# A mixture-of-experts kernel: the instruction order of the first chunk's steps, with decoding, attention and x0's split moved

## The chip, the cores and the metric

One core of a Trainium2 chip. The metric is device time in microseconds (us) of one execution; the times shown are of single executions and their median. Engines: TensorE (PE), VectorE (DVE), ScalarE (ACT), GpSimd (POOL), and SyncE (SP), which only issues loads and stores here. Each engine runs its queue in order.

## The reference

```python
x = attention(q, k, v)              # 4 batches, 8 heads, 576 positions, 64 wide;
                                    # causal, each position sees the last 64
x = x.reshape(2304, 512)            # tokens by heads
h = x @ w_in                        # 512 -> 2048
g = where(h >= 1, h, where(h <= -1, 0, (h + 1)**2 / 4))
y = g @ w_out                       # 2048 -> 512
e, weight = top-1 of softmax(y @ w_gate + bias[modality])
out = weight * (relu(y @ w1[e]) @ w2[e])     # 8 experts, 512 -> 1024 -> 512
```

`w_in` and `w_out` come as 64-bit floats; the kernel turns their words into 32-bit floats itself.

## The kernel before

The 2304 tokens are taken in six chunks of 384. A chunk has 16 steps `f`, one for each 128 columns of the hidden layer: `l1(c, f)` multiplies the chunk's x by block f of `w_in` into PSUM, `relu` (two ACT instructions) and `act2` (one on DVE) make g of it, and `l2(c, f)`, two steps later, adds g times block f of `w_out` to three sums. While a chunk c is worked on, attention of chunk c+1 is made, six blocks of 64 positions with all heads. After the last chunk tokens are routed and the experts run. From the second chunk on weights and x are split into a high part and a rounded rest, and products are made of three matmuls.

The first chunk, `step0(f)` (L1048), has more to do than the others. Weights must be decoded, a pair of blocks at a time: `dec_load` (SP) fetches the pair's words, `dec_abs` (two on ACT), `dec_clamp` (four on DVE) and `dec_merge` (four on DVE) make 32-bit floats. `turn[f]` says which pairs step f decodes: one pair, and two in the steps of `TWICE` (L207); there are 16 pairs, the first of them ahead of step 0. `dec_load(p + 3)` is issued in the step that merges pair p, whose place it takes. Up to step 8 whole 32-bit weights and x0 are used (`l1_whole`, L476); from step `FS` = 9 on split ones, and from `FJ` = 10 on each step also makes the second chunk's first layer, `l1(1, f)`. `split_hi` (ACT) and `split_lo` (DVE) split a weight block; `soon` (L234 to L239) says in which step. `split_x0(j)` splits half j of x0: a copy on ACT (L349), the rest on DVE (L350).

Attention of the second chunk's blocks, numbered 6 to 11 here, is a pipeline over the steps: block 6 has phase 0 in step 1, phase 1 in step 2, and so on, block 7 one step later.

- Phase 0: `att_mm` (scores on PE, L370), `att_loads` (SP fetches later k and q), `att_max` (masked maxima, four on DVE, L385), `att_exp` (four exponentials with sums on ACT, L395).
- Phase 1: `load_v` (SP); `att_norm`, which is `att_sum` (two small instructions on DVE, L407 and L408) and `att_scale` (four on ACT for these blocks, L416).
- Phase 2: `att_tr`, four transposes on PE (L425) and a copy of the result, ts, on ACT (L430).
- Phase 3: `att_pv`, multiplication by v on PE (L447); `att_x`, xh on ACT (L467) and the rounded rest xl on DVE (L468).

Scores, transposes and products share three PSUM buffers ("aux"); s and ts have two buffers each, q, k and v two.

In the first chunk the order on PE, DVE, ACT and POOL is the order of the calls in `step0`, by `manual_schedule`; SP's order is written out by hand throughout. After the chunk a planner with estimated costs sets the order of DVE, ACT and POOL, and from step 3 of the second chunk PE's is by hand again.

Of the kernel before, what the change touches and what calls it, by code (L numbers as in the profile page):

```python
# [71 lines left out]
def moe_kernel(ctx, tc, qT, kT, v, w_in, w_out, mod, wg, wgT, mbias, w1, w2, cst, tri, empty, out, spec):  # L72
# [131 lines left out]
    PRE = 3  # L204
    LAG = 2
    FS, FJ = 9, 10
    TWICE = (3, 6)  # L207

    def part(kind, f, lo):
        return parts[kind, f][0][:, lo * WB : (lo + 1) * WB]  # L210
# [22 lines left out]
    NPR = len(pairs)  # L233
# [1 line left out]
    for f in range(FS, NF - 1):  # L235
        soon.setdefault(f + 1, []).append((1, f))
    soon[NF - 1].append((1, NF - 1))
    for f, kf in ((13, (0, 0)), (14, (0, 1)), (14, (0, 2)), (15, (1, 0))):
        soon[f].append(kf)  # L239
    turn, p = [], 1  # L240
    for f in range(NF + 1):
        turn.append(list(range(p, min(p + 1 + (f in TWICE), NPR))))
        p += len(turn[-1])
# [24 lines left out]
    def dec_abs(p, us=(0, 1)):  # L268
        if p < NPR:
            for u in us:  # L270
                dts.setdefault(p, {})[u] = tile_of([P, DM], f"dt{p}_{u}", I32, tag="y", bufs=4)
                A.activation(dts[p][u].bitcast(F32), words(p, u)[1].bitcast(F32), AF.Abs)

    def dec_clamp(p, us=(0, 1)):
        if p < NPR:
            t = dts[p]
            for u in us:
                tf = t[u].bitcast(F32)
                V.tensor_scalar(tf, tf, c0, c1, op0=ALU.max, op1=ALU.min)
            for u in us:  # L280
                V.tensor_scalar(t[u], t[u], 5, 2, op0=ALU.logical_shift_left, op1=ALU.logical_shift_right)

    def dec_merge(p, us=(0, 1)):
        if p < NPR:
            t = dts[p]
            for u in us:
                V.scalar_tensor_tensor(
                    t[u], words(p, u)[1], -0x40000000, t[u], op0=ALU.bitwise_and, op1=ALU.bitwise_or
                )
            for u in us:  # L290
                w = raw_home(p, u)
                V.scalar_tensor_tensor(
                    w, words(p, u)[0], 29, t[u], op0=ALU.logical_shift_right, op1=ALU.bitwise_or
                )
                whole[pairs[p][u]] = w.bitcast(F32)
# [46 lines left out]
    def split_x0(j):  # L342
        if not j:
            hi = [tile_of([P, 2 * WB], f"x0h{n}", F32R, tag=f"T{NF + 10 + n}") for n in range(2)]
            hi = [t[:, : KH * CT].rearrange("p (k n) -> p k n", k=KH) for t in hi]
            xs[0] = (hi, tile_of([P, KD, CT], "x0l", F32R, tag="xl", bufs=2))
        hi, lo = xs[0]
        ks = slice(j * KH, (j + 1) * KH)
        A.copy(hi[j], whole_x[0][:, ks])  # L349
        V.tensor_tensor(lo[:, ks], whole_x[0][:, ks], hi[j].bitcast(F32), op=ALU.subtract)  # L350
# [50 lines left out]
    def att_norm(i):  # L401
        att_sum(i)
        att_scale(i)

    def att_sum(i):
        sm = at[i][1]
        V.tensor_scalar_add(sm, sm, 1e-9)  # L407
        V.reciprocal(sm, sm)  # L408

    def att_scale(i):  # L410
        s, sm = at[i]
        s = s[:, :, : window(i)[0]]
        if BPC - 1 <= i < 2 * BPC:
            w = window(i)[0]
            for hp in range(KD):
                A.activation(s[:, hp, :w], s[:, hp, :w], AF.Copy, scale=sm[:, hp : hp + 1])  # L416
            return
        G.tensor_tensor(s, s, bc(sm, 2, window(i)[0]), op=ALU.mult)  # L418

    def att_tr(i):  # L420
        s, _ = at[i]
        n = window(i)[0]
        pt = aux([P, KD, P], f"pt{i}")
        for hp in range(KD):
            T.transpose(pt[:n, hp, :], s[:, hp, :n], C["ident"])  # L425
        if i < BPC:
            ts = lend(8 + i, 1).rearrange("p (k n) -> p k n", k=KD)
        else:
            ts = tile_of([P, KD, P], f"ts{i}", tag="ts", bufs=2)
        (V.tensor_copy if i < BPC - 2 else A.copy)(ts[:n], pt[:n])  # L430
        at[i] = ts

    def att_pv(i):
        o = 0
        if i < BPC:
            xo = ps.tile([P, KD, BLK], F32, name=f"xo{i}", tag="h", bufs=2)
        elif i < PAIRED:
            xo = aux([P, KD, BLK], f"xo{i}")
        else:
            o = i % GB  # L440
            xo = xos[i - 1] if o else aux([P, KD, GT], f"xo{i}")
        ts = at.pop(i)
        vt = vs.pop(i)
        w = window(i)[0]
        for hp in range(KD):
            for a in range(2):
                T.matmul(  # L447
                    xo[a * D : (a + 1) * D, hp, o * BLK : (o + 1) * BLK],
                    vt[:w, (2 * hp + a) * D : (2 * hp + a + 1) * D],
                    ts[:w, hp, a * BLK : (a + 1) * BLK],  # L450
                    start=True,
                    stop=True,
                )
        xos[i] = xo

    def att_x(i):
        xo = xos.pop(i)
        c, n = divmod(i, BPC)
        dst = slice(n * BLK, (n + 1) * BLK)
        if i >= PAIRED:  # L460
            xos.pop(i + 1)
            dst = slice(n * BLK, n * BLK + GT)
        if c == 0:
            A.copy(whole_x[0][:, :, dst], xo)
            return
        xh, xl = xs[c]
        A.copy(xh[:, :, dst], xo)  # L467
        V.tensor_tensor(xl[:, :, dst], xo, xh[:, :, dst].bitcast(F32), op=ALU.subtract)  # L468
# [14 lines left out]
    def l1(c, f):  # L483
        if (c, f) not in hs:
            if c == 1 and f >= FJ:
                hs[c, f] = aux([P, CT], f"h{c}_{f}")
            else:
                hs[c, f] = ps.tile([P, CT], F32, tag="h", name=f"h{c}_{f}", bufs=2)
            if c == 0 and f < FS:
                l1_whole(f, slice(0, CT))  # L490
        h = hs[c, f]
        n = 0
        for k in range(KD if c or f >= FS else 0):
            xh, xl = xs[c]
            xh = xh[:, k, :] if c else xh[k // KH][:, k % KH, :]
            for a, b in ((0, xh), (0, xl[:, k, :]), (1, xh)):
                T.matmul(h, wi(f, a)[:, k, :], b, start=n == 0, stop=n == 3 * KD - 1)  # L497
                n += 1

    def relu(c, f):  # L500
        h = hs[c, f]
        u = tile_of([P, CT], f"u{c}_{f}", tag="u", bufs=2)
        A.activation(u, h, AF.Relu, bias=half, scale=0.5)  # L503
        A.activation(u, u, AF.Square)  # L504
        us[c, f] = u
# [542 lines left out]
    def step0(f):  # L1048
        split0 = f - 1 >= FS
        join = f >= FJ  # L1050
        at_step = {f - st: BPC + k for k, st in enumerate(FIRST)}
        if f == NF - 3:
            free.extend(f"T{NF + k}" for k in (14, 15))
        if f >= 1:
            act2(0, f - 1)
            if split0:
                gsplit_hi(0, f - 1, us[0, f - 1])
        if f - 1 >= FJ:
            act2(1, f - 1)
        for kf in soon.get(f, []):  # L1060
            split_lo()
        if split0:
            gsplit_lo(0, f - 1, us[0, f - 1])
        for p in turn[f]:
            dec_clamp(p)
            dec_merge(p)
        if 3 in at_step:
            att_pv(at_step[3])
            att_x(at_step[3])
        if 2 in at_step:  # L1070
            att_tr(at_step[2])
        if 1 in at_step:
            load_v(at_step[1])
        if 0 in at_step:
            att_mm(at_step[0])
            att_loads(at_step[0])
        for p in turn[f]:
            dec_load(p + 3)
        l1(0, f)
        relu(0, f)  # L1080
        for p in turn[f + 1][:1]:
            dec_abs(p)
        if 1 in at_step:
            att_norm(at_step[1])
        if 0 in at_step:
            att_max(at_step[0])
            att_exp(at_step[0])
        if f in (FS - 2, FS - 1):
            split_x0(f - FS + 2)
        if join:  # L1090
            l1(1, f)
            relu(1, f)
        if f >= LAG:
            l2(0, f - LAG)
        for p in turn[f + 1][1:]:
            dec_abs(p)
        for kf in soon.get(f + 1, []):
            split_hi(kf)
        if f == FS - 1:
            token_bias()  # L1100
        if f == NF - 1:
            free.extend(f"T{NF + k}" for k in (10, 11))
            hold_back(gs[0, f - 1][0].bitcast(F32))
            wgb.append(tile_of([P, E, DM], "wgb", tag="dec"))
            SP.dma_start(
                wgb[0].rearrange("p e d -> p (e d)"),
                wgT.rearrange("(o e) d -> o (e d)", o=1).broadcast_to([P, E * DM]),
            )
# [7 lines left out]
    for n in range(len(its) + LAG):  # L1116
        c, f = its[n] if n < len(its) else (NC, n - len(its))
# [151 lines left out]
```

## Time and profile before

| what | us |
|---|---|
| median of 3 executions | 736.45 |
| lowest, highest | 735.43, 738.32 |
| the profiled execution, its own time | 735.82 |
| its span in the trace | 734.2 |
| PE busy in the span | 717.1 (98%) |
| DVE busy | 474.2 (65%) |
| ACT busy | 390.1 (53%) |

The profile is of one execution; its span is a little shorter than the time, which takes in start and end. Busy time of PE is that of pipelined matmuls, whose ends are modelled. The first chunk's steps 1 to 9 lie between 24 and 87 us, its last six until 126 us. In rows, `dt<-dec` on ACT is `dec_abs`, L279 and L281 are `dec_clamp`, L287 and L292 `dec_merge`, `g<-u,h` is `act2`, `u<-h,half` is the first instruction of `relu`.

### The profile page before, as it was taken

The page shows a single profiled execution, that of the slowest core. Times are in us where ns is not written, and L with a number is a line of the kernel's source. Part 1 is how long each engine was busy: PE and PEld are TensorE (multiplying, and loading weights), DVE is VectorE, ACT ScalarE, POOL GpSimd, SP SyncE. Part 2 cuts the span into 40 slices and gives each one's busy share as a digit, 9 for nine tenths or more (in the row PEclk, how much of TensorE's full clock was granted, in tenths as well). Part 3 has the DMA queues.
Part 4 walks back from the last instruction along what each step waited for, and adds up shares of the span by engine and source line. Part 5 has one row for each costly group of instructions (what it writes and reads, how often), then busy time and mean ns, then how long its engine had stood idle before and what let it go on. Part 6 is the DMA issues. An engine that isn't in the chain of part 4 may idle for free. (4 is left out here: it accounts for less than half of the span.)

```text
span 734.2 us, 12536 instructions
## 1 busy us (share of the span) xinstructions
PE 717.1 (98%) x4217; PEld 625.5 (85%) x4217; DVE 474.2 (65%) x1439; ACT 390.1 (53%) x942; POOL 127.0 (17%) x185
## 2 busy tenths in 40 slices
PE   8899999999999999999999999999999999999994
PEld 6555689888998989888989898999989989898984
DVE  5999897797397528852696638866775545453600
ACT  6777778666545535554555445645444544453511
POOL 3200000113001201120111502031058322201010
PEclk9999999999999999999999999999999999999998
DMA  9997413322121203220310015245455754444310
GB/s 327 334 346 258 147 55 127 118 66 80 52 86 59 80 15 108 73 80 16 108 59 29 2 41 171 67 93 191 158 137 171 232 181 155 159 159 160 115 43 7
DMA packets 48570, 89.26 MB, mean 122 GB/s; under 512 B 6976, under 2 KB 16320, under 8 KB 48368
## 3 DMA queue, kind: packets, MB, share of 16 engines
q1 hardware_dynamic: 44064, 78.36, 32.3%
q0 software_dynamic: 4288, 9.79, 4.6%
q8 instruction: 35, 0.57, 0.3%
q14 instruction: 39, 0.32, 0.1%
q10 hardware_dynamic: 144, 0.22, 0.1%
HBM read 78.89 MB, written 9.87 MB: 121 GB/s over the span
## 5 line engine op out<-in xcount | busy, mean ns | idle before, releaser
L497 PE MATMUL h<-xh,w 128*128 128x384 f32 x640 | 179.4, 341 | 0.0
L549 PE MATMUL py<-w,gh 128*128 128x512 f32 x522 | 162.1, 393 | 0.0
L497 PEld LDWEIGHTS h<-xh,w 128*128 128x128 f32 x640 | 117.1, 188 | 2.3
L549 PEld LDWEIGHTS py<-w,gh 128*128 128x128 f32 x522 | 96.6, 188 | 16.2
L497 PE MATMUL h<-xl,w 128*128 128x384 f32 x320 | 107.4, 336 | 0.0
L796 DVE TENSOR_TENSOR e<-wr,e 128x512 fp32r<-128x512 f32 x112 | 74.7, 690 | 45.2 <-ACT e L795 43.2
L549 PE MATMUL py<-w,gl 128*128 128x512 f32 x261 | 102.7, 396 | 0.0
L858 PE MATMUL hp<-zh,e 128*128 128x384 f32 x384 | 100.9, 336 | 0.0
L503 ACT ACTIVATE u<-h,half 128x384 f32<-128x384 f32 x96 | 55.5, 578 | 82.3 <-PE h L497 70.8
L873 PE MATMUL yo<-e,hm 128*128 128x512 f32 x348 | 99.0, 394 | 0.0
L517 DVE SCALAR_TENSOR_TENSOR u<-u,h 128x384 f32<-128x384 f32 x81 | 44.7, 552 | 68.3 <-ACT u L504 67.8
L603 DVE CUSTOM_DVE_ANT_0 prod<-y,wgb 128x512 f32<-128x512 f32 x120 | 85.3, 710 | 1.3
L529 ACT CAST gh<-u 128x384 fp32r<-128x384 f32 x81 | 41.6, 514 | 67.5 <-DVE u L517 29.1
L795 ACT CAST e<-wr 128x512 fp32r<-128x512 f32 x112 | 66.0, 616 | 18.4 <-DMA wr<-in_w 18.2
L873 PEld LDWEIGHTS yo<-e,hm 128*128 128x128 f32 x348 | 64.2, 188 | 12.4
L858 PEld LDWEIGHTS hp<-zh,e 128*128 128x128 f32 x384 | 69.6, 188 | 0.8
L418 POOL TENSOR_TENSOR s<-s,sm 128x512 f32<-128x512 f32 (+1 forms) x24 | 26.2, 1093 | 222.4 <-DVE sm L408 158.1
L858 PE MATMUL hp<-zl,e 128*128 128x384 f32 x192 | 64.3, 335 | 0.0
L534 DVE TENSOR_TENSOR gl<-u,gh 128x384 fp32r<-128x384 f32 x81 | 45.5, 562 | 26.7 <-ACT gh L529 25.7
L497 PEld LDWEIGHTS h<-xl,w 128*128 128x128 f32 x320 | 60.2, 188 | 1.9
L549 PEld LDWEIGHTS py<-w,gl 128*128 128x128 f32 x261 | 48.9, 188 | 10.4
L395 ACT ACTIVATE s<-s,mx 128x128 f32<-128x128 f32 (+1 forms) x120 | 45.9, 385 | 11.7 <-DVE mx L385 11.7
(218 smaller groups left out, 1049.5 us busy)
## 6 DMA issues: line engine op xcount, KB each, us to landing
wr<-in_w SPq DMA_DIRECT2D x112, 256.0 KB, 2.9
q<-in_qT SPq DMA_DIRECT2D x32, 256.0 KB, 3.4
dec<-in_w_in SPq DMA_DIRECT2D x16, 512.0 KB, 5.5
dec<-in_w_out SPq DMA_DIRECT2D x16, 512.0 KB, 4.3
v<-in_v SPq DMA_DIRECT2D x27, 256.0 KB, 3.0
k<-in_kT SPq DMA_DIRECT2D x15, 384.0 KB, 4.7
yd<-y SPq DMA_DIRECT2D x18, 256.0 KB, 2.2
wgb<-in_wgT SPq DMA_DIRECT2D x1, 2048.0 KB, 6.9
```

The costliest lines, as they stand in the source:

```text
L395: A.activation(s[:, hp, :n], s[:, hp, :n], AF.Exp, bias=mx[:, hp : hp + 1], scale=-1.0, accum_out=sm[:, hp : hp + 1],)
L497: T.matmul(h, wi(f, a)[:, k, :], b, start=n == 0, stop=n == 3 * KD - 1)
L503: A.activation(u, h, AF.Relu, bias=half, scale=0.5)
L517: V.scalar_tensor_tensor(g, u, 1.0, h, op0=ALU.min, op1=ALU.max)
L529: A.copy(gh, u)
L534: V.tensor_tensor(gl, u, gh.bitcast(F32), op=ALU.subtract)
L549: T.matmul(ys[c][t], a[:, sl], wo(f, b), start=f == first and n == 0, stop=f == last and n == 2)
L603: V.tensor_tensor_reduce(prod, yt[t], wgb[0][:, e, :], 1.0, 0.0, ALU.mult, ALU.add, lg[:, t, e : e + 1])
L795: A.copy(wpart(i, p, 0), t)
L796: V.tensor_tensor(wpart(i, p, 1), t, wpart(i, p, 0).bitcast(F32), op=ALU.subtract)
L858: T.matmul(hp, w1s(i, f, k, a), b[:, k, :], start=n == 0, stop=n == 3 * KD - 1)
L873: T.matmul(yo, a[f][:, sl], w2s(i, f, b), start=n == 0, stop=n == 3 * NF2 - 1)
```

## The change

In `step0` the calls get another order. On DVE the clamps come first, then `att_sum`, then the rest xl of `att_x`, then the merges of the first pair; a second pair is decoded whole after them. On PE the order becomes: product with v, first layer of the first chunk, scores, transposes, (first layer of the second chunk), second layer. On ACT `att_scale` comes ahead of `relu` and `dec_abs`, the copy of the transposes after them. On SP the order is kept. Step 3 decodes one pair, no longer two, so pairs 5 to 7 and those from 9 on are decoded a step later than before. x0 is split in steps 6 and 7, formerly 7 and 8. Four weight blocks that the second chunk needs are split in steps 14, 14, 15, 15, formerly 13, 14, 14, 15.

```diff
-    TWICE = (3, 6)
+    TWICE = (6,)
...
-    for f, kf in ((13, (0, 0)), (14, (0, 1)), (14, (0, 2)), (15, (1, 0))):
+    for f, kf in ((14, (0, 0)), (14, (0, 1)), (15, (0, 2)), (15, (1, 0))):
...
-        for p in turn[f]:
+        dec_clamp(*turn[f][:1] or [NPR])
+        if 3 in at_step:
+            att_pv(at_step[3])
+        if 1 in at_step:
+            att_sum(at_step[1])
+        if 3 in at_step:
+            att_x(at_step[3])
+        if 1 in at_step:
+            att_scale(at_step[1])
+        dec_merge(*turn[f][:1] or [NPR])
+        for p in turn[f][1:]:
             dec_clamp(p)
             dec_merge(p)
-        if 3 in at_step:
-            att_pv(at_step[3])
-            att_x(at_step[3])
-        if 2 in at_step:
-            att_tr(at_step[2])
+        l1(0, f)
+        relu(0, f)
+        for p in turn[f + 1][:1]:
+            dec_abs(p)
         if 1 in at_step:
             load_v(at_step[1])
         if 0 in at_step:
...
         for p in turn[f]:
             dec_load(p + 3)
-        l1(0, f)
-        relu(0, f)
-        for p in turn[f + 1][:1]:
-            dec_abs(p)
-        if 1 in at_step:
-            att_norm(at_step[1])
+        if 2 in at_step:
+            att_tr(at_step[2])
         if 0 in at_step:
             att_max(at_step[0])
             att_exp(at_step[0])
-        if f in (FS - 2, FS - 1):
-            split_x0(f - FS + 2)
+        if f in (FS - 3, FS - 2):
+            split_x0(f - FS + 3)
```

## Rows read from the trace of the kernel before

**Rows 1.** Windows: stretch, busy us of each engine, PEclk, DMA share, GB/s.

```profile
27.63:87.46 59.83, 54.50 (x278) 31.38 (x276) 55.04 (x163) 45.29 (x128) 5.40 (x5) 1.00 0.77 281
87.46:125.91 38.45, 38.45 (x198) 34.81 (x196) 34.55 (x67) 29.05 (x57) 1.14 (x4) 1.00 0.26 100
```

**Rows 2.** Waits of PE to 140 us, then after it: total, times, longest.

```profile
PE pt L425 <- ACT s L416: 4.6, 3, 3.1
...
PE h L497 <- DVE x0l L350: 0.7, 1, 0.7
...
PE rt L907 <- ACT hr L901: 0.3, 1, 0.3
```

**Rows 3.** Timeline of PE: start us, length us, engine, line, operation.

```profile
36.91 1.20 PE L425 MATMUL pt<-cs,s 128*128 128x128 f32 x4 [3.09 <-ACT s L416]
...
53.19 0.69 PE L447 MATMUL xo<-ts,v 128*64 128x64 f32 x16
...
54.38 1.07 PE L370 MATMUL sc<-k,q 128*128 128x128 f32 x8
55.28 2.75 PE L476 MATMUL h<-x,raw 128*128 128x384 f32 x8
57.86 2.74 PE L543 MATMUL py<-raw,g 128*128 128x512 f32 x6
60.53 0.69 PE L447 MATMUL xo<-ts,v 128*64 128x64 f32 x16
...
81.46 0.69 PE L447 MATMUL xo<-ts,v 128*64 128x64 f32 x16
...
87.46 0.73 PE L497 MATMUL h<-x0h,w 128*128 128x384 f32 x1
```

**Rows 4.** Timeline of DVE, from steps 2, 3, 4 and 7.

```profile
32.30 0.76 DVE L279 TENSOR_SCALAR dt<-dt 128x512 f32<-128x512 f32 x2
...
33.64 1.29 DVE L287 SCALAR_TENSOR_TENSOR dt<-dec,dt 128x512 int32<-128x512 int32 x2
...
36.04 0.17 DVE L407 TENSOR_SCALAR sm<-sm 128x4 f32<-128x4 f32 x1
...
36.34 0.26 DVE L385 CUSTOM_DVE_ANT_0 s<-sc,cs 128x128 f32<-128x128 f32 x1
...
37.16 0.55 DVE L517 SCALAR_TENSOR_TENSOR g<-u,h 128x384 f32<-128x384 f32 x1
...
50.45 0.42 DVE L468 TENSOR_TENSOR xl<-xo,xh 128x256 fp32r<-128x256 f32 x1
...
76.74 0.96 DVE L350 TENSOR_TENSOR x0l<-x,x0h 128x768 fp32r<-128x768 f32 x1 [2.83 <-ACT x0h L349]
```

**Rows 5.** Timeline of ACT, from steps 3 to 5 and 7.

```profile
46.72 0.39 ACT L395 ACTIVATE s<-s,mx 128x128 f32<-128x128 f32 x1
...
48.27 0.35 ACT L467 CAST xh<-xo 128x256 fp32r<-128x256 f32 x1
48.52 0.57 ACT L430 COPY ts<-pt 128x512 f32<-128x512 f32 x1
50.72 0.58 ACT L503 ACTIVATE u<-h,half 128x384 f32<-128x384 f32 x1 [1.63 <-PE h L476]
...
51.76 1.23 ACT L272 ACTIVATE dt<-dec 128x512 f32<-128x512 f32 x2
52.88 1.28 ACT L416 ACTIVATE s<-s,sm 128x128 f32<-128x128 f32 x4
...
58.06 0.58 ACT L503 ACTIVATE u<-h,half 128x384 f32<-128x384 f32 x1 [1.85 <-PE h L476]
...
75.89 0.82 ACT L349 CAST x0h<-x 128x768 fp32r<-128x768 f32 x1
```

**Rows 6.** DMA issues, 10 to 60 us: times, KB each, us to landing.

```profile
q<-in_qT SPq DMA_DIRECT2D x7, 256.0 KB, 6.7
```

**Rows 7.** Windows, after the last matmul of the kernel.

```profile
730.00:734.20 4.20, 0.00 (x0) 0.00 (x0) 0.00 (x0) 0.00 (x0) 0.00 (x0) 0.50 0.00 0
```

## The prediction

> **What bounds the kernel now.** I read the windows first: which engine is full, stage by stage. From 87 us on TensorE (PE) has no gap [rows 1], and after 140 us it waits 0.3 us in all [rows 2]. So time won or lost in the first chunk of tokens, the stretch that the change reorders, comes out at the end almost unchanged, as long as nothing later starts to wait. In the first chunk PE is busy 54.50 of 59.83 us [rows 1]. The list of waits names the gaps: 4.6 us in three waits of the transposes for ScalarE's scaling, the longest 3.1 us, and 0.7 us for the rest of x0 [rows 2]. Some 1.5 us more hide in three groups of transposes that lasted 1.20 us because they ran head by head behind the scaling (one of the three: [rows 3]); a step without a wait gives multiplication by v and transposes together 1.19 us (53.19 to 54.38), about half for each. About 7 us is therefore all that an order can win here.
>
> The timeline shows the cause. The sums of a block stand on VectorE (DVE) behind the step's merges (36.04, after merges from 33.64) [rows 4]; the scaling and the next step's transposes wait for them, and behind the transposes wait the scores and the first-layer block.
>
> **Durations,** as distances between starts, of one profiled execution. PE, a step of 7.34 us (53.19 to 60.53): by v and transposes about 0.60 each, scores 0.90, l1 2.58, l2 2.67 [rows 3]. DVE: clamps of a pair 1.34, merges 2.40, sums 0.30, maxima of a block 0.82, rest 0.4 and x0's rest 0.9 (0.42 and 0.96 less overlap), g 0.47 (0.55 less the 0.08 by which neighbours overlap) [rows 4]. ScalarE (ACT): the four exponentials 1.55, xh 0.25, ts 0.5, relu 1.04 and starting 2.78 after l1 (55.28 to 58.06), abs of a pair 1.12, scaling 1.18, half of x0 0.72 (0.82 less overlap) [rows 5].
>
> **The change, walked through.** Total work is unchanged on every engine; only waits move. I carry the end of each link to the next; blocks of the second chunk are numbered 6 to 11.
>
> *Steps 2 to 5: a gain.* In step 2 the clamps end at 33.64, the sums of block 6 at 33.94 instead of 36.34, the merges at 36.34, the maxima of block 7 at 37.16, where they ended before. ACT: scaling 35.1, relu 36.2, abs 37.3, exponentials of block 7 38.9. PE no longer waits until 36.91 [rows 3]: it runs step 3 (l1, scores, transposes, l2: 6.75) from 33.8 to 40.5. But its next instruction, block 6 by v, needs ts of block 6, which now stands on ACT behind step 3's scaling, relu and abs: g 37.6, clamps 39.0, sums of block 7 39.3, scaling 40.5, relu 41.5, abs 42.7, ts 43.2. So PE waits from 40.5 to 43.3: the wait of 3.1 us comes back as one of 2.8. From there a step is PE's own 7.34, since each link of relu, abs and ts (l1 start + 2.78 + 1.04 + 1.12 + 0.5, so 6.1 after the step's start) comes before its end. Step 5 begins at 50.6, where it began at 53.19: **2.6 us won.** Taking the second pair out of step 3 leaves DVE at 5.7 us a step, which hides under PE; without that it would be 9.5 and not hide.
>
> *Steps 6 to 8: a loss.* Steps 6 and 7 begin on PE at 58.0 and 65.3; step 7 has no scores and is 6.44 us long, so PE is free at 71.8. DVE in step 6 has two pairs and, new here, half of x0. ACT, step 5: relu 55.1, abs 56.2, ts 56.7, exponentials of block 10 58.3, abs of the second pair 59.4, xh 59.6. DVE: maxima 56.1 (they wait for the transposes two blocks back, which free their buffer and now come late in the step), g 56.6, clamps 57.9, sums 58.7, rest 60.1 (it waits for xh), merges 62.5, second pair (1.34 + 2.40) 66.2, maxima of block 11 67.0. ACT: its exponentials 68.2, x0's half 68.9. DVE: x0's rest 69.9, then step 7: g 70.4, clamps 71.7, sums of block 11 72.0. ACT: scaling 73.2, relu 74.3, abs 75.4, ts of block 10 75.9. PE needs that ts for its next instruction: it waits from 71.8 to 76.0, **4.2 us**, where today there is no wait. DVE waited for x0's half before too, 2.83 us [rows 4], but after the sums of block 11; now it waits ahead of them, and that puts about 3 of the 4.2 us on the path.
>
> *Step 9.* Step 8 ends at 76.0 + 6.44 = 82.4, and step 9 on PE, today 6.0 (81.46 to 87.46 [rows 3]), loses its wait of 0.7 for x0, which is now split early. Step 10 begins at 87.7 instead of 87.46. **Sum: about 0.3 us later,** that is 2.6 won in the first steps, some 1.3 in the waits of steps 7 and 9 that go, and 4.2 given back in between.
>
> *The rest.* The decoding of the last pair moves from step 12 to 13: in PE's full stretch DVE gets 3.74 us more out of the stage before, and is idle 3.9 us there now (38.45 less 34.55 [rows 1]). I take it as hidden; uncovered it would cost up to those 3.74. One split goes from step 13 to 15, about 0.6 us of each engine, under the same cover; its buffers come free in the same order. On SP the loads of q come after scores that now follow l1, and those of the decoder queue behind them. The tightest is q of block 8: issued near 28.5 as before, used by 36.4 instead of 37.95, and a load of q takes 6.7 us in the median [rows 6]. Should it be 1 or 2 us late, the 2.8 us wait behind it takes that up: bounds 0 and 0, below. GpSimd gets nothing new in the chunk. The planner's order after the chunk may shift; PE had next to nothing to wait for there, so I set it at 0, with about 1 us either way.
>
> The profiled execution took 735.82, its span 734.2; 0.3 more is 736.1 on its scale. The median shown lies 0.6 above it: **736.8.**
>
> **The rivals.** (a) *No wait at step 8.* PE would keep the 2.6 and the 1.3: 4.2 less than my sum, 732.6 at the median. It wants ts of block 10 by 71.8. For it: no wait of today is longer than 3.1 us [rows 2], and the chain from 56.1 to 75.9 has some 17 links, each of which could be a little shorter. Against it: queues run in written order here, and even with the x0 pieces out of the chain (some 2.9 us) a wait of about 1.3 us stays. Chance 0.11; partial cases lie in my range.
>
> (b) *The clock falls in the wait of step 8: slower.* The granted clock is 1.00 through the waits of today, the 3.1 us one included [rows 1], that is 2.4 GHz; after PE's last matmul of the kernel it reads 0.50, that is 1.2 GHz [rows 7]. The new wait is longer than the one that kept the clock. If it loses it, matmuls of step 8 run at half speed for a while: nothing at the least, and if all of step 8 did, its 6.44 us again, 743.2. It decides from 3.4 us of work at half speed upwards. Against it: the wait is one, with dense work on both sides. Chance 0.08. The Trainium skill ("TensorE: Matmul & The Clock Gate", section "HAM oscillation") has this as a rule: waits throw the engine back to half rate, and the work behind them starts cold. By that rule the sum would lie toward 743.2; by the row of the 3.1 us wait it stays at 736.8, and I hold to the row.
>
> (c) *DVE gets behind in steps 13 to 15.* If its idle 3.9 us lie where the decoding cannot use them, PE waits for the last splits: up to 3.74 + 0.6, giving 741.1. Against it: DVE is about a microsecond ahead of today in step 10. Chance 0.04.
>
> That the new order isn't taken can't be: today's queues of this chunk follow the written order in every row that I read.
>
> **How the numbers follow.** Forecast (within 2 us or so of 736.8) and its partial cases 0.77; (a) 0.11, (b) 0.08, (c) 0.04. 3.7 us, 0.5%, is about what a measurement tells from no change, the runs of before lying 2.9 us apart. (a) just passes it: faster 0.12, with a little from partial cases. (b) and (c) pass it only in part: slower 0.09. Same 0.79. The range, 733.0 to 740.0, takes the wait at step 8 from nearly nothing to 3 us more than worked out, or half of it with half a step cold, and the spread of runs.
>
> **What would show it.** Right: PE waits of about 3 us at block 6 by v and about 4 us at block 10 by v, both for ts on ACT; none left at the transposes; the first wait for x0 gone; step 5 near 50.6 and step 10 near 87.7 to 88.0; PE full from there on. Wrong: no wait at block 10 by v (then a), a clock under 1.00 between 70 and 90 us (b), or PE gaps after 110 us (c).

## The result, and the profile after

The changed kernel took 739.95 us (median of 8, 738.22 to 742.59), the kernel before 736.45; the ratio is 1.0051, with an interval from 1.0034 to 1.0068. **It became slower by about half a per cent.** Forecast was 736.8. The span of the profiled execution grew from 734.2 to 738.1 us.

PE's waits up to 145 us (total, times, longest), which answer to [rows 2]:

```profile
PE xo L447 <- ACT ts L430: 7.9, 2, 4.5
PE warm L942 <- DVE wz L939: 1.3, 1, 1.3
PE sc L370 <- DMA lent<-in_qT: 0.7, 1, 0.7
PE h L476 <- ACT x L464: 0.2, 1, 0.2
```

The transposes no longer wait, nor does step 9 for x0. Two waits take their place, both of the product with v, both for ts on ACT. The timeline of PE (answering to [rows 3]) shows where they stand:

```profile
38.31 2.74 PE L543 MATMUL py<-raw,g 128*128 128x512 f32 x6
44.51 1.12 PE L447 MATMUL xo<-ts,v 128*64 128x64 f32 x16 [3.46 <-ACT ts L430]
45.56 3.96 PE L476 MATMUL h<-x,raw 128*128 128x384 f32 x8
...
53.31 0.69 PE L447 MATMUL xo<-ts,v 128*64 128x64 f32 x16
...
71.64 2.74 PE L543 MATMUL py<-raw,g 128*128 128x512 f32 x6
78.83 1.12 PE L447 MATMUL xo<-ts,v 128*64 128x64 f32 x16 [4.45 <-ACT ts L430]
79.89 3.87 PE L476 MATMUL h<-x,raw 128*128 128x384 f32 x8
...
86.70 0.69 PE L447 MATMUL xo<-ts,v 128*64 128x64 f32 x16
...
91.68 0.74 PE L497 MATMUL h<-x0h,w 128*128 128x384 f32 x1
```

Behind each wait the same instructions are longer than elsewhere: by v 1.12 instead of 0.69, the first-layer block 3.96 and 3.87 instead of 2.75 [rows 3]. Step 4, from 44.51 to 53.31, lasted 8.80 us, step 8, from 78.83 to 86.70, 7.87; undisturbed they are 7.3 and 6.4 by the prediction's durations, and they measured 7.25 and 6.41 in the kernel with both waits filled (below). The windows say why (stretch, busy time of the engines, then the granted clock, DMA share, GB/s):

```profile
40.00:50.00 10.00, 6.54 (x34) 4.00 (x32) 8.45 (x26) 7.37 (x23) 0.00 (x0) 0.83 0.85 318
...
76.00:78.00 2.00, 0.00 (x0) 0.00 (x0) 1.53 (x3) 1.97 (x5) 0.00 (x0) 1.00 0.10 12
78.00:80.00 2.00, 1.17 (x17) 1.05 (x17) 0.46 (x1) 2.00 (x4) 0.00 (x0) 0.64 0.84 287
80.00:82.00 2.00, 2.00 (x4) 1.09 (x5) 2.00 (x4) 0.37 (x2) 0.79 (x2) 0.51 0.58 234
82.00:84.00 2.00, 2.00 (x10) 1.29 (x9) 2.00 (x6) 0.21 (x1) 0.48 (x1) 1.00 0.00 0
...
91.68:130.00 38.32, 38.32 (x197) 34.73 (x196) 35.79 (x71) 29.06 (x57) 1.16 (x4) 1.00 0.35 127
```

The clock fell from 2.4 to 1.2 GHz around both waits and came back within the step: around the second by these rows, around the first it read 0.54 from 46 to 48 us and 1.00 from 48 to 50. From 91.68 us on PE is full, as before [rows 1].

The chain that makes the second wait is the forecast one. DVE (answering to [rows 4]) and ACT (to [rows 5]) in steps 6 and 7:

```profile
71.75 0.96 DVE L350 TENSOR_TENSOR x0l<-x,x0h 128x768 fp32r<-128x768 f32 x1 [1.80 <-ACT x0h L349]
72.63 0.55 DVE L517 SCALAR_TENSOR_TENSOR g<-u,h 128x384 f32<-128x384 f32 x1
...
74.44 0.16 DVE L407 TENSOR_SCALAR sm<-sm 128x4 f32<-128x4 f32 x1
```

```profile
74.91 1.28 ACT L416 ACTIVATE s<-s,sm 128x128 f32<-128x128 f32 x4 [2.92 <-DVE sm L408]
76.09 0.56 ACT L503 ACTIVATE u<-h,half 128x384 f32<-128x384 f32 x1
...
77.11 1.20 ACT L272 ACTIVATE dt<-dec 128x512 f32<-128x512 f32 x2
78.21 0.57 ACT L430 COPY ts<-pt 128x512 f32<-128x512 f32 x1
```

**The account.** Step 10 begins at 91.68, where it began at 87.46 [rows 3]: 4.2 us. This execution entered step 2 about 0.7 us later (its clamps begin at 33.04, those of [rows 4] at 32.30). That is scatter of the start: the same 0.74 us stand ahead of step 0 already (PE's first matmuls of L476 begin at 21.29, formerly 20.55), and the other profiles of the new order enter step 2 between 32.34 and 33.29. The slow clock took 1.5 (8.80 less 7.3) and 1.5 (7.87 less 6.4). Some 0.5 is left, which is about the forecast sum of 0.3.

### The profile page after: what moved, and what is told of

Its sections match the earlier page's. It is cut to its first block, busy times and chain, and to the rows that moved or that the text cites. A ratio compares the mean times of both kernels' runs of the same rounds, so it can differ in the third digit from the quotient of the medians.

```text
span 738.1 us, 12531 instructions
## 1 busy us (share of the span) xinstructions
PE 719.2 (97%) x4217; PEld 628.0 (85%) x4217; DVE 474.9 (64%) x1439; ACT 389.8 (53%) x942; POOL 126.6 (17%) x185
```

## The experiments

The theory after the result: the waits are as worked out, and the difference is the clock. The rivals: the waits cost more than worked out by themselves; or DVE bounds the stage, so that no order of it could win. Each kernel ran beside the kernel before, in two sets; its median was 736.21 in the first (both waits filled in part, x0 back, and the two kernels with ts ahead) and 736.23 in the second (the others). The changed kernel itself ran again in the second set alone.

**The changed kernel again.**

> The changed kernel once more, beside the three below on the same chip: waits of about 3.5 and 4.5 us for ts, the granted clock at half after both, and some 3.5 us above the kernel before (739.7). Were the clock's fall a chance of the one profiled execution, the profile would show 1.00 from 40 to 85 us here.

Measured: 740.42 us, ratio 1.0057 (1.0044 to 1.0070). Waits of 3.30 and 4.40 us; PEclk 0.83 in the window from 40 to 50 and 0.83 from 70 to 90. Step 4 lasted 8.94 us (44.60 to 53.54), step 8 8.55 (79.01 to 87.56). The clock's fall is no chance of one execution: in all thirteen of the changed kernel the granted clock, averaged over the execution, is 0.988 to 0.995.

**Both waits filled in part, then almost whole.** Small matmuls go into the tile that the product with v then overwrites, 28 and 36 of them in the first kernel; in the second the numbers are 48 and 68:

```diff
+    FILL = {6: 28, 10: 36}
+
     def att_pv(i):
...
             xo = aux([P, KD, BLK], f"xo{i}")
+            for _ in range(FILL.get(i, 0)):
+                T.matmul(xo[:, :2, :], ones16, ones16.rearrange("p (a b) -> p a b", a=2), start=True, stop=True)
```

> The changed kernel with 28 small matmuls ahead of block 6 by v and 36 ahead of block 10 by v, into the PSUM tile that the product overwrites; nothing else is moved, nothing of the computation is left out. Theory (the clock falls in the two waits): the matmuls take 2 to 4 us of each wait, the granted clock stays at 1.00 from 40 to 90 us, steps 4 and 8 last 7.3 and 6.4 us instead of 8.8 and 7.9, and the time is about 2.9 us under the changed kernel, near 737.0 us, 0 to 1 us above the kernel before. Rival (the waits themselves are longer than worked out, the clock is a side effect): the time stays within 1 us of the changed kernel, near 740.

Measured: 738.02 us, ratio 1.0025 (1.0014 to 1.0035), 1.0 above the expected 737.0; about half of the loss is left. The first filling left 1.72 us of waiting and the clock stayed up; the second left 2.43 us, and the clock fell all the same. PE's timeline and windows of this kernel:

```profile
40.38 1.73 PE L442 MATMUL xo<-ones 128*128 128x128 f16 x28
43.83 0.69 PE L451 MATMUL xo<-ts,v 128*64 128x64 f32 x16 [1.72 <-ACT ts L430]
44.44 2.85 PE L480 MATMUL h<-x,raw 128*128 128x384 f32 x8
...
71.98 2.17 PE L442 MATMUL xo<-ones 128*128 128x128 f16 x36
76.58 1.12 PE L451 MATMUL xo<-ts,v 128*64 128x64 f32 x16 [2.43 <-ACT ts L430]
77.64 3.85 PE L480 MATMUL h<-x,raw 128*128 128x384 f32 x8
...
84.42 0.69 PE L451 MATMUL xo<-ts,v 128*64 128x64 f32 x16
```

```profile
40.00:50.00 10.00, 8.28 (x70) 5.82 (x69) 9.30 (x35) 9.47 (x28) 0.00 (x0) 1.00 0.79 289
...
77.00:78.00 1.00, 1.00 (x15) 0.88 (x12) 0.71 (x1) 1.00 (x3) 0.00 (x0) 0.50 1.03 422
```

So one of the two losses is undone in it, and the other not: step 8 still lasts 7.84 us (76.58 to 84.42). That called for the longer filling.

> The kernel with small matmuls in both waits, now 48 and 68 of them (0.06 us each by the shorter filling: 2.9 and 4.1 us), so that nearly all of both waits is filled; nothing of the computation is left out. Theory (the clock): the granted clock stays at 1.00 after the second wait too, step 8 lasts 6.4 us instead of 7.8, and the time falls by 1.4 us below the shorter filling, to about 736.6, within 1 us of the kernel before. Rival (the loss of step 8 has another cause than the clock, such as the x0 copies beside it): step 8 stays at 7.8 us and the time at 738.

Measured: 736.85 us, ratio 1.0007 (0.9999 to 1.0016): no difference to the kernel before that can be told. The waits left are 0.65 and 0.64 us, and the clock stays at 1.00 in both windows:

```profile
50.95 0.69 PE L451 MATMUL xo<-ts,v 128*64 128x64 f32 x16
...
71.86 3.96 PE L442 MATMUL xo<-ones 128*128 128x128 f16 x68
76.45 0.69 PE L451 MATMUL xo<-ts,v 128*64 128x64 f32 x16 [0.64 <-ACT ts L430]
77.07 2.85 PE L480 MATMUL h<-x,raw 128*128 128x384 f32 x8
...
82.86 0.69 PE L451 MATMUL xo<-ts,v 128*64 128x64 f32 x16
...
87.83 0.74 PE L501 MATMUL h<-x0h,w 128*128 128x384 f32 x1
```

```profile
40.00:50.00 10.00, 9.35 (x89) 6.88 (x88) 9.26 (x35) 9.46 (x28) 0.00 (x0) 1.00 0.79 291
...
70.00:90.00 20.00, 19.36 (x152) 13.61 (x151) 17.91 (x39) 12.80 (x26) 1.28 (x2) 1.00 0.37 132
```

Nothing useful was moved, the product with v begins no earlier relative to the work before it (filling and wait together still take 3.5 and 4.6 us), and 3.6 us (740.42 less 736.85, the same set) are back, of the 4.2 by which the changed kernel lies above the kernel before (740.42 less 736.23). This settles it: the clock costs 3.6 us, and the order alone about 0.6, which these runs can't tell from nothing. All eleven executions of this kernel average a granted clock of 0.996 to 0.998, above every one of the changed kernel.

**x0 split in steps 7 and 8 again.**

```diff
-        if f in (FS - 3, FS - 2):
-            split_x0(f - FS + 3)
+        if f in (FS - 2, FS - 1):
+            split_x0(f - FS + 2)
```

> The changed kernel with x0 split in steps 7 and 8 again; all else as changed. By the walk through the queues the wait ahead of block 10 by v shrinks from 4.5 to 1.6 us, since VectorE no longer waits for ScalarE's half of x0 ahead of the sums of block 11. Theory (waits and clock): the wait gives 2.9 us back, and 1.4 more as the clock does not fall there any more; the wait of 3.2 us in step 4 and its clock loss stay: some 4.3 us under the changed kernel, near 735.6. Rival (the second pair of step 6 alone makes that wait): it stays over 3.5 us, and the time within 1 us of the changed kernel.

Measured: 736.31 us, ratio 1.0000 (0.9990 to 1.0011), some 0.7 above the expected 735.6. The second wait shrinks to 1.65 us and leaves the clock at 1.00; the first stays, 3.51 us, and the clock falls behind it, for longer than before (step 4 lasts 10.3 us, to 54.27):

```profile
43.96 1.12 PE L447 MATMUL xo<-ts,v 128*64 128x64 f32 x16 [3.51 <-ACT ts L430]
45.02 5.46 PE L476 MATMUL h<-x,raw 128*128 128x384 f32 x8
...
54.27 0.69 PE L447 MATMUL xo<-ts,v 128*64 128x64 f32 x16
...
76.99 0.68 PE L447 MATMUL xo<-ts,v 128*64 128x64 f32 x16 [1.65 <-ACT ts L430]
```

The longer step 4 is not what shortens the second wait: with both waits filled step 4 lasted 7.25 us, and filling and second wait still took 4.6. Moving x0 forward is thus what stretched the second wait past 4 us: it put ACT's half of x0, and DVE's wait for it, ahead of the sums of block 11.

**The second pair back in step 3.** The edit is `TWICE = (3, 6)`.

> The changed kernel with a second pair decoded in step 3 as well, as before the change; all else as changed. The walk gives waits of 3.8, 1.1 and 4.5 us (blocks 6, 7 and 10 by v): 1.8 us above the changed kernel, near 741.5, the clock falling in the two long ones as it does there. Rival (the second pair of step 3 hides under TensorE, as it did before the change): no difference to the changed kernel.

Measured: 740.43 us, ratio 1.0057 (1.0044 to 1.0070), the same as the changed kernel beside it. The first wait did grow, to 3.88 us, but the one at block 7 did not come: step 4 runs at the low clock (0.50 from 44 to 49 us) and is 9.6 us long (44.35 to 53.98), which leaves DVE that much more time; that this is why the wait stayed away was not shown. I expected 1.8 us and missed; the time is the rival's. What that pair would cost with the clock kept was not tried.

**PE's order back.** Transposes, scores, first-layer block, as before; the rest as changed.

```diff
-        l1(0, f)
-        relu(0, f)
-        for p in turn[f + 1][:1]:
-            dec_abs(p)
+        if 2 in at_step:
+            att_tr(at_step[2])
         if 1 in at_step:
             load_v(at_step[1])
...
             dec_load(p + 3)
-        if 2 in at_step:
-            att_tr(at_step[2])
+        l1(0, f)
+        relu(0, f)
+        for p in turn[f + 1][:1]:
+            dec_abs(p)
```

> The changed kernel with the first-layer block, relu and abs behind transposes and scores again, as before the change; DVE's new order, the earlier scaling, x0 in steps 6 and 7 and the single pair of step 3 stay. The walk gives waits of 1.0 us (transposes of block 6) and 3.3 us (block 10 by v): 3.0 us less waiting than the changed kernel, and 1.5 more with the clock kept in step 4, so 735.2, or 736.6 at most; the clock after the second wait may fall or not. Rival (the new place of the first-layer block is what wins the 2.6 us of steps 2 to 5): step 5 begins on TensorE 2 us or more later than in the changed kernel without its clock loss, and the time is 738 or above.

Measured: 735.23 us, ratio 0.9987 (0.9978 to 0.9996), as expected. PE waits 0.74 us at the transposes of block 6, and 3.28 us at block 10; here that wait left the clock at 1.00 in the profiled execution:

```profile
35.13 1.21 PE L425 MATMUL pt<-cs,s 128*128 128x128 f32 x4 [0.74 <-ACT s L416]
...
49.66 0.69 PE L447 MATMUL xo<-ts,v 128*64 128x64 f32 x16
...
73.85 0.69 PE L447 MATMUL xo<-ts,v 128*64 128x64 f32 x16 [3.28 <-ACT ts L430]
```

```profile
70.00:90.00 20.00, 16.72 (x95) 11.77 (x94) 17.93 (x38) 13.17 (x27) 1.27 (x2) 1.00 0.35 128
```

That execution, 734.10 us with an average clock of 0.997, is the fastest of the eleven; the others average 0.991 to 0.996, so the clock may have fallen in some of them, which no trace shows.

Step 5 begins on PE at 49.66, not later than in the changed kernel (53.31; 50.95 with both waits filled and the clock kept) but earlier: the rival is out. The gain of steps 2 to 5 comes from sums and scaling ahead of the merges and from the single pair (which of the two was not separated); putting the first-layer block first added the wait of step 4, since its relu and abs then stand with the scaling ahead of ts.

**ts ahead of the scaling.** Two kernels aim at what makes the waits. In the first the scaling is called behind the transposes; in the second abs, too, comes behind them, and step 6's second pair comes behind the maxima.

```diff
         if 3 in at_step:
             att_x(at_step[3])
-        if 1 in at_step:
-            att_scale(at_step[1])
         dec_merge(*turn[f][:1] or [NPR])
...
         if 2 in at_step:
             att_tr(at_step[2])
+        if 1 in at_step:
+            att_scale(at_step[1])
```

> The changed kernel with the scaling of a block behind the transposes' copy in ScalarE's queue (order xh, relu, abs, ts, scaling, exponentials); nothing else moved. Theory: both long waits come from ts standing behind a scaling that waits for VectorE; the walk gives waits of 0.9 us (block 6) and 1.2 us (block 10) in place of 3.2 and 4.5, no fall of the clock, and about 8.4 us under the changed kernel, near 731.5, some 5 us under the kernel before. Rival (VectorE is the bound of the stage, and the wait only moves): another wait of 3 us or more appears in steps 4 to 9, and the time stays above 736.

Measured: 730.69 us, ratio 0.9922 (0.9908 to 0.9936), 0.8 under the expected 731.5. Waits of 0.73 us (block 6) and 1.25 us (block 10), clock 1.00 in every window from 20 to 130 us.

```diff
-        if 1 in at_step:
-            att_scale(at_step[1])
         dec_merge(*turn[f][:1] or [NPR])
-        for p in turn[f][1:]:
-            dec_clamp(p)
-            dec_merge(p)
         l1(0, f)
         relu(0, f)
-        for p in turn[f + 1][:1]:
-            dec_abs(p)
...
-        for p in turn[f]:
+        for p in turn[f][:1]:
             dec_load(p + 3)
         if 2 in at_step:
             att_tr(at_step[2])
+        for p in turn[f + 1][:1]:
+            dec_abs(p)
+        if 1 in at_step:
+            att_scale(at_step[1])
         if 0 in at_step:
             att_max(at_step[0])
+        for p in turn[f][1:]:
+            dec_clamp(p)
+            dec_merge(p)
+            dec_load(p + 3)
+        if 0 in at_step:
             att_exp(at_step[0])
```

> As the one before, and the transposes' copy also ahead of abs, and step 6's second pair behind the maxima of block 11 on VectorE. The walk finds no wait on TensorE left from step 1 to 15: about 10 us under the changed kernel, 7 under the kernel before, near 729.5. Rival (VectorE is the bound): waits appear in steps 10 to 15 or at the start of the second chunk, as VectorE gets the same work in less time, and the time is 732 or more.

Measured: **729.22 us, ratio 0.9906 (0.9891 to 0.9922)**, 7.0 us under the kernel before and the best of all. In its first chunk PE has no gap left:

```profile
27.63:80.20 52.57, 52.57 (x279) 31.61 (x277) 50.22 (x155) 43.98 (x126) 8.95 (x5) 1.00 0.82 296
80.20:119.00 38.80, 38.80 (x202) 35.28 (x201) 35.90 (x71) 29.31 (x57) 1.16 (x4) 1.00 0.36 131
```

DVE is busy 50.22 of 52.57 us in it and does not bound it, nor does a wait of more than 0.3 us appear later. The rival "DVE is the bound" is out.

## Why the prediction was wrong

- *The walk through the queues* held. In the kernel with both waits filled, whose waits are as long and whose clock does not fall, step 5 begins at 50.95 and step 10 at 87.83; the walk said 50.6 and 87.7. Its time lies 0.6 us above the kernel before, where the sum said 0.3. That 736.85 meets the 736.8 so closely is in part luck: the sum started from 736.45 for the kernel before, and the two sets gave 736.2.
- *Steps 2 to 5.* The wait came back at block 6 by v, as said, with 3.5 us in place of 2.8 (it was mis-sized by 0.7): PE was free at 41.05 and got ts at 44.51. Of the 2.6 us to be won there the clock took back 1.5; step 5 began at 53.31, or 52.6 without the later entry, not at 50.6.
- *Steps 6 to 8.* The wait of 4.2 us was 4.45, for the reason given, and the x0 pieces account for 2.8 of it (4.45 less 1.65).
- *Step 9 and the rest* were right: no wait for x0, nothing hidden came out later, PE full from step 10 on.
- **The step that failed is rival (b)**, "I hold to the row": that a wait of 3.1 us had kept the clock was taken as evidence for a wait of 4.2, and rival (b) was looked for in step 8 alone, with a chance of 0.08. Step 4's wait, which the same text puts at 2.8 us, was counted as free of it, and it came out longer than the 3.1 that the row covered. The sum thus had no term for the clock. What the runs showed in its place are two falls: by the step lengths 1.5 us each in the changed kernel's first profile, 1.6 and 2.1 in its second, and together 3.6 by the medians of two kernels of one set. Its price for the rival, 6.4 us "if all of step 8" ran at half speed, was three to four times what one fall cost. That 739.95 still lies inside the stated range, at its very edge, is owed to the room left there for a longer wait, or for half of it with half a step cold. The 0.5% that the prediction took as about what a measurement can tell from no change was too coarse: these 0.51% stand clear of it, with an interval from 0.34 to 0.68%.
- *The row itself was one execution.* The profiled execution of the kernel before averages a granted clock of 0.996. Of the 46 that ran beside the experiments 31 average 0.994 or less, down to 0.991, and the seven at 0.991 have a median of 737.3 us, about 1 us above the rest. Where the clock was low in them no trace shows; that the wait of 3.1 us keeps it every time was never established.
- The Trainium skill ("TensorE: Matmul & The Clock Gate", section "HAM oscillation") says that long waits of TensorE for its data throw the engine back to half rate, so that the work behind them starts cold. The traces agree for 3.46 and 4.45 us in the first profile and for 3.30 and 4.40 in the second, and it was the better guide than the one row; but 3.28 us in the profiled execution with PE's order back kept 1.00, as the 3.1 us in that of the kernel before had.

## What to carry to other kernels

When an order is changed so that small waits become one long one, price the work behind the wait at both clock levels: the walk had the waits about even, and the clock made the difference. A queue in which something needed next (ts) stands behind something that waits for another engine (the scaling) shows in a walk through the queues with durations from the trace, and putting it ahead won 9.7 us against the changed kernel (740.42 to 730.69), and 11.2 (to 729.22) with abs and the second pair moved behind it too; some 3.6 of that is the clock. Filling a wait with matmuls into a tile that is overwritten anyway is a quick test of whether the clock is the cause.

## What the runs showed that was not expected

- The length of a wait alone did not tell whether the clock falls: 2.43 us behind 36 small matmuls lost it, 3.28 and 3.1 us behind the second-layer block kept it, 3.30, 3.46 and 4.45 us behind the same block lost it. Each of these is one profiled execution, and by their average clocks executions of one kernel differ.
- The fall can come after work has begun again: in the second profile of the changed kernel the product with v after the wait of 3.30 us still took its usual 0.69 us, and the first-layer block behind it 4.54 in place of 2.75:

```profile
44.60 0.69 PE L447 MATMUL xo<-ts,v 128*64 128x64 f32 x16 [3.30 <-ACT ts L430]
45.21 4.54 PE L476 MATMUL h<-x,raw 128*128 128x384 f32 x8
```

- One fall did not always cost the same: step 4 lasted 8.80 us in the changed kernel, 10.3 with x0 moved back, at nearly the same wait (3.46 and 3.51 us). What decides this was not tried.
